# Opening of a Fourier and feed-forward kernel: R's copy on ScalarE, a weight fold moved ahead of the first product, GpSimd's sums held

## The chip, the cores and the metric

The kernel runs on 1 core of one Trainium2 chip. The metric is the device time of one execution in microseconds (us). "Span" below is the time from the first to the last instruction in the trace of one execution; the time of the same execution is some 2 us more. Every run also lists its mean granted TensorE clock, as a share of full speed.

The engines are named as in the profile: PE (TensorE), PEld (its weight loads), DVE (VectorE), ACT (ScalarE), POOL (GpSimd), SP (SyncE).

## The reference

```python
def _attn_ref(x):                      # x: 8 x 3008 x 256, float32
    X = np.fft.fft(x, axis=1)
    X = np.fft.fft(X, axis=2)
    return X.real

def _moe_ref(x, w_in, w_out):          # w_in: 256 x 2048, w_out: 2048 x 256
    h = x @ w_in
    g = h * np.cos(h)
    return g @ w_out
```

The output of the first is the input of the second, 24,064 rows.

## The kernel before

The channel transform is folded into the weights: `w_in` times a cosine matrix gives `Wc`, times a sine matrix gives `Ws` ("a fold" below, 4 passes of 128x512). The sequence transform makes, for each batch, a cosine part R and a sine part I by small DFT products; both lie in rings `Rr` and `Ir` in SBUF. A step of the feed-forward part fills a PSUM bank `H` with the contribution of one extra channel (ScalarE, `Rb` times a column of `wex`), adds `Rr` times `Wc` and `Ir` times `Ws` on TensorE, and goes on with the cosine and the second matrix. A step takes about 4.75 us on TensorE in the steady stage (from one first product to the next, as near 200 us), and some 6 to 7 us in the opening, where folds lie between. VectorE's "odd folds" are something else: sums and differences of parts of `x`, made ahead of the small DFT products.

The opening, in program order for each engine:

```python
    warm(60)                       # 60 products on ones
    ...
    fold_mm(0, 1)                  # first sine fold
    fold_mm(0, 0)                  # first cosine fold
    ...
    fold_copy(0, 1)                # ScalarE: Ws, first quarter
    take_last(0); turn_last(0)     # its last row, turned into wex[0]
    fold_copy(0, 0)
    first_x.first_part("pC")       # DFT of the extra channel
    first_R.first_part("pA")       # DFT of R, in two halves
    ...
    first_R.part(1)
    warm(6)
    fold_now("o2 O2 o1 O0 J0")     # VectorE's odd folds of x
    add_O(2, 0)
    halve_now(1, VO[3])            # the last three odd folds
    first_R.plus_copy()            # VectorE: R from PSUM into the ring
```

The rest is a list of events, each with a time, that are sorted and then issued:

```python
    for t, fn in (
        (0.5, lambda: fold_mm(1, 1)),            # second sine fold
        ...
        (0.88, lambda: first_I.early("pB", "M")),  # I's DFT
        (0.95, lambda: fold_copy(1, 1)),
        (0.955, lambda: take_last(1)),
        (0.96, lambda: turn_last(1)),            # second bias row, wex[1]
        ...
    ):
        at(t, fn)
    for k in range(4):
        at(-0.1, lambda k=k: sum_weights(0, k))  # GpSimd
    at(-1.5 * T, load_ext)                       # T is 4.8
```

Two transfers of the opening: The bias row is the last row of a folded `Ws` quarter, 512 numbers, turned on end so that each of 128 partitions gets 4 of them. It goes out from GpSimd (a software queue):

```python
    def turn_last(q):
        with nc.allow_non_contiguous_dma(reason="one row turned"):
            pin(nc.gpsimd.dma_start(out=wex[q], in_=turned[q][127:128, :]))
```

Steps 0 and 1 need `wex[0]`, steps 2 and 3 need `wex[1]`, and so on. The other transfer takes one channel of `x` for every row of every batch, element by element, from SyncE; GpSimd's memset of `x1` goes ahead of it:

```python
    def load_ext():
        x1 = spool.tile([128, HALF + 1], FP, tag="rx", bufs=1, name="x1")
        ...
        pin(nc.gpsimd.memset(x1[0 : 4 * NB, 0:768], 0.0))
        ...
        with nc.allow_non_contiguous_dma(reason="one channel"):
            copy(rows[1][:, 0:1], HALF, [[SEQ * ND, NB], [-HALF * ND, 2], [1, 1]])
            copy(rows[0][:, 0:768], 0, [[HALF * ND, 2 * NB], [ND, 768], [1, 1]])
            copy(rows[1][:, 1:768], HALF - 1, [[HALF * ND, 2 * NB], [-ND, 767], [1, 1]])
```

Later, near 115 and 134 us, that extra channel gets its own small DFT, twice ("the extra-channel part"):

```python
    def clear_ext():
        ps = state["ext"] = bank("H")
        pin(nc.vector.memset(ps[0:40, 0:NQ], 0.0))
    ...
        at(s * T + 2.905, clear_ext)
        at(s * T + 4.75, lambda: dft_ext(kodd))
        at((s + 1) * T + 1.46, lambda: ext_side(kodd))
```

## Time and profile before

| | before |
|---|---|
| time, median of 3 runs (range) | 1936.52 us (1935.99 to 1937.42) |
| span and clock of the profiled run | 1931.7 us, 0.998 |
| first product with R, with I (PE's timeline) | 33.49, 40.88 us |
| products with R of steps 1, 2, 3 | 43.56, 49.73, 57.02 us |
| granted clock | 0.5 for 3.41 us twice (from 21.1 and from 34.75 us) |

The prediction below shows the views that carry it. The first is a row of the table of stretches (stretch, length, busy time of PE, PEld, DVE, ACT, POOL, granted clock, DMA share, GB/s):

```profile
40.00:60.00 20.00, 18.43 (x62) 11.06 (x61) 13.56 (x20) 14.64 (x26) 13.61 (x19) 1.00 1.67 5
```

The DMA share is the highest of the opening while only 5 GB/s move: this is the element-by-element load. PE is idle for 1.6 us of the 20.

The second is the timeline of the kernel before (start, duration, engine, line, operation, out<-in, count; in brackets the idle time ahead of it and what ended that). SPq rows are SyncE's DMA issues:

```profile
25.61 0.63 POOL L348 DMA_DIRECT2D wex<-wl  x1 [2.43 <-ACT wl L310]
31.08 17.53 SPq L156 DMA_DIRECT2D x<-in_x_dram  x3
31.24 0.99 ACT L310 ACTIVATE H<-Rb,wex 128x256 f32<-128x256 f32 x2 [1.75 <-DMA wex<-wl]
39.73 0.58 POOL L348 DMA_DIRECT2D wex<-wl  x1 [5.58 <-ACT wl L310]
48.69 0.99 ACT L310 ACTIVATE H<-Rb,wex 128x256 f32<-128x256 f32 x2 [1.52 <-DVE G L304]
49.73 1.13 PE L298 MATMUL H<-Rr,Wc 128*128 128x256 f32 x4
```

The first bias row goes out at 25.61, and ScalarE's fill for step 0 waits for it until 31.24. The second goes out at 39.73, while SyncE is still issuing the element loads (31.08 to 48.6). The trace also keeps the moments at which the 16 parts of a transfer land; the last part of the second row lands at 48.61. ScalarE's fill for step 2 starts at 48.69, and the product with R that needs it at 49.73. The profile puts the fill's wait down to VectorE; in the program the fill waits for an earlier use of its bank by VectorE, done at 45.86, and for this row. The instruction that it names, VectorE's subtraction `G<-E,H` of step 1, ended at 48.67, but it reads the bank of step 1, which is still in use at 51.49. ScalarE's own wait instruction for the row's semaphore stands at 48.63 in the trace. So it was the row.

PE's timeline at the extra-channel part:

```profile
114.96 0.49 PE L298 MATMUL H<-MC,xe 95*40 95x95 f32 x4 [0.76 <-DVE H L722]
116.23 1.18 PE L298 MATMUL H<-MC,xe 95*40 95x95 f32 x12 [0.78 <-DVE xe L375]
133.75 2.10 PE L298 MATMUL H<-MC,xe 95*40 95x95 f32 x16 [1.09 <-DVE H L722]
```

PE stands still for 2.63 us in three waits, between very short products.

### The profile page before, as it was taken

The page shows a single profiled execution, that of the slowest core. Times are in us where ns is not written, and L with a number is a line of the kernel's source. Part 1 is how long each engine was busy: PE and PEld are TensorE (multiplying, and loading weights), DVE is VectorE, ACT ScalarE, POOL GpSimd, SP SyncE. Part 2 cuts the span into 40 slices and gives each one's busy share as a digit, 9 for nine tenths or more (in the row PEclk, how much of TensorE's full clock was granted, in tenths as well). Part 3 has the DMA queues.
Part 4 walks back from the last instruction along what each step waited for, and adds up shares of the span by engine and source line. Part 5 has one row for each costly group of instructions (what it writes and reads, how often), then busy time and mean ns, then how long its engine had stood idle before and what let it go on. Part 6 is the DMA issues. An engine that isn't in the chain of part 4 may idle for free.

```text
span 1931.7 us, 28919 instructions
## 1 busy us (share of the span) xinstructions
PE 1908.5 (99%) x9000; PEld 1652.0 (86%) x9000; DVE 1456.5 (75%) x2367; ACT 1519.5 (79%) x2993; POOL 1521.4 (79%) x2044
## 2 busy tenths in 40 slices
PE   8999999999999999999999999999999999999998
PEld 4778888888888888888888888888888888888887
DVE  6788877777777777777777777777777777777777
ACT  3767788888878887888778787788878887877886
POOL 5779888898888888888889898888878676555554
PEclk9999999999999999999999999999999999999999
DMA  9523311312123122311232113311122110100101
GB/s 200 39 65 69 59 40 28 65 28 56 24 48 57 36 40 45 56 35 37 43 68 33 40 23 61 52 40 32 29 30 36 19 20 17 18 12 12 22 9 25
DMA packets 259970, 80.59 MB, mean 42 GB/s; under 512 B 240393, under 2 KB 243256, under 8 KB 259816
## 3 DMA queue, kind: packets, MB, share of 16 engines
q1 hardware_dynamic: 248456, 48.65, 15.1%
q0 software_dynamic: 9184, 29.83, 8.3%
q8 instruction: 72, 1.18, 0.2%
q14 instruction: 82, 0.67, 0.1%
q10 hardware_dynamic: 2176, 0.26, 0.1%
HBM read 36.72 MB, written 24.69 MB: 32 GB/s over the span
## 4 chain that ended last, share of the span: by engine, by line
PE 87%; DVE 5%; ACT 5%; issue 1%; POOL 1%; DMA 0%; SPq 0%; DVEq 0%; POOLq 0%
PE H L298 34%; PE pC L298 15%; PE pD L298 15%; PE pB L298 15%; PE pA L298 7%; ACT G L310 1%; DVE G L845 1%; DVE G L304 1%; ACT E L310 1%; ACT M L310 1%; ACT z L310 1%; DVE v L304 1%; ACT H L310 0%; DVE M L304 0%; DVE o L375 0%
## 5 line engine op out<-in xcount | busy, mean ns | idle before, releaser
L307 POOL TENSOR_TENSOR G<-G 128x256 f32<-128x256 f32 x1500 | 1084.6, 734 | 357.8 <-DVE G L845 280.5
L845 DVE SCALAR_TENSOR_TENSOR G<-H,G 128x512 f32<-128x512 f32 x376 | 259.2, 689 | 222.0 <-ACT G L310 219.3
L304 DVE TENSOR_TENSOR G<-H,G 128x512 f32<-128x512 f32 x376 | 259.7, 691 | 216.9 <-ACT G L310 213.7
L298 PE MATMUL H<-Rr,Wc 128*128 128x256 f32 x1504 | 388.5, 381 | 3.1 <-DVE Rr L609 2.1
L298 PE MATMUL H<-Ir,Ws 127*128 127x256 f32 x1504 | 387.8, 379 | 3.5 <-ACT E L310 2.7
L298 PE MATMUL pC<-G,WT 128*128 128x256 f32 x1504 | 387.6, 380 | 0.8 <-DVE u L304 0.7
L310 ACT ACTIVATE H<-Rb,wex 128x256 f32<-128x256 f32 x752 | 359.9, 479 | 25.6 <-DVE G L845 9.8
L310 ACT ACTIVATE G<-H 128x512 int32<-128x512 f32 x376 | 223.8, 595 | 178.9 <-DVE G L304 178.0
L310 ACT ACTIVATE E<-H 128x512 f32<-128x512 f32 x376 | 223.8, 595 | 166.2 <-PE H L298 164.8
L298 PEld LDWEIGHTS H<-Ir,Ws 127*128 127x128 f32 x1504 | 283.4, 189 | 48.3 <-ACT E L310 7.3
L298 PEld LDWEIGHTS pC<-G,WT 128*128 128x128 f32 x1504 | 285.1, 190 | 43.1 <-PE H L298 1.5
L298 PEld LDWEIGHTS H<-Rr,Wc 128*128 128x128 f32 x1504 | 281.1, 190 | 44.2 <-issue 4.6
L310 ACT ACTIVATE G<-G,halfpi 128x512 f32<-128x512 f32 x376 | 269.3, 716 | 3.6 <-DVE G L304 3.4
L304 DVE TENSOR_TENSOR M<-G,M 128x512 f32<-128x512 f32 x376 | 257.6, 685 | 0.0
L304 DVE TENSOR_TENSOR G<-E,H 128x512 f32<-128x512 f32 x376 | 255.3, 679 | 1.6 <-PE H L298 1.5
L845 DVE SCALAR_TENSOR_TENSOR G<-G,M 128x512 f32<-128x512 f32 x376 | 254.4, 677 | 0.5 <-ACT M L310 0.5
L310 ACT ACTIVATE M<-M,halfpi 128x512 f32<-128x512 f32 x376 | 245.6, 653 | 0.0
L298 PE MATMUL pB<-G,WT 128*128 128x256 f32 x752 | 225.0, 381 | 1.4 <-POOL G L307 1.3
L310 ACT ACTIVATE M<-G 128x512 int32<-128x512 f32 x376 | 223.7, 595 | 0.0
L298 PE MATMUL pA<-G,w 128*128 128x256 f32 x752 | 223.7, 379 | 0.0
L298 PE MATMUL pD<-G,w 128*128 128x256 f32 x752 | 223.7, 379 | 0.0
L298 PE MATMUL pB<-G,w 128*128 128x256 f32 x752 | 223.7, 379 | 0.0
(164 smaller groups left out, 2070.9 us busy)
## 6 DMA issues: line engine op xcount, KB each, us to landing
out_dram<-ot SPq DMA_DIRECT2D x496, 32.0 KB
xl<-in_x_dram SPq DMA_DIRECT2D x64, 192.0 KB
e<-e POOLq DMA_DIRECT2D x22, 384.0 KB, 4.9
o<-o POOLq DMA_DIRECT2D x22, 381.0 KB, 4.9
out_dram<-ot SPq DMA_DIRECT2D x256, 2.0 KB
Rb<-r SPq DMA_DIRECT2D x10, 376.0 KB
w<-in_moe_w_in_dram SPq DMA_DIRECT2D x4, 512.0 KB
out_dram<-ot SPq DMA_DIRECT2D x64, 28.0 KB
```

Of the source, the lines that this page charges most:

```text
L298: nc.tensor.matmul(out_, lhsT=lhsT, rhs=rhs, start=start, stop=stop, skip_group_check=True)
L304: pin(nc.vector.tensor_tensor(out=o, in0=a, in1=b, op=op))
L307: pin(nc.gpsimd.tensor_tensor(out=o, in0=a, in1=b, op=op))
L310: pin(nc.scalar.activation(out=o, in_=i, func=func, **kw))
L845: nc.vector.scalar_tensor_tensor(out=o, in0=h, scalar=TWO_PI, in1=c, op0=ALU.mult, op1=ALU.mult)
```

## The change

It means to start the first product earlier and to shorten what lies between it and the first product with I: ScalarE copies R, so that VectorE's last folds are not ahead of it; the second sine fold takes the place of the six warming products; GpSimd's weight sums do not start while VectorE does its last folds (a copy of one element that depends on `O[3]` holds them); twelve more warming products keep the clock; a load changes its place; and the extra-channel DFT comes later, behind the next step's product, with its bank cleared on TensorE.

```diff
@@ loads
     load_mats(0)
+    load_w1(1)
     load_mats(1)
-    load_w1(1)
@@ clear_ext
-        pin(nc.vector.memset(ps[0:40, 0:NQ], 0.0))
+        whole_bank("ext")
@@ opening
-    warm(60)
+    warm(72)
 ...
     first_R.part(1)
-    warm(6)
+    fold_mm(1, 1)
+    first_R.plus_sum()
     fold_now("o2 O2 o1 O0 J0")
     add_O(2, 0)
     halve_now(1, VO[3])
-    first_R.plus_copy()
+    hold = spool.tile([128, 8], FP, tag="xg", bufs=1, name="hold")
+    pin(nc.gpsimd.tensor_copy(out=hold[0:1, 0:1], in_=O[3][0:1, 0:1]))
@@ events
-        (0.5, lambda: fold_mm(1, 1)),
+        (0.1, lambda: fold_copy(1, 1)),
+        (0.11, lambda: take_last(1)),
 ...
         (0.88, lambda: first_I.early("pB", "M")),
-        (0.95, lambda: fold_copy(1, 1)),
-        (0.955, lambda: take_last(1)),
-        (0.96, lambda: turn_last(1)),
+        (0.12, lambda: turn_last(1)),
 ...
-        at(-0.1, lambda k=k: sum_weights(0, k))
+        at(0.13, lambda k=k: sum_weights(0, k))
@@ plan_ext
-        at(s * T + 2.905, clear_ext)
-        at(s * T + 4.75, lambda: dft_ext(kodd))
-        at((s + 1) * T + 1.46, lambda: ext_side(kodd))
+        at(s * T + 5.6, clear_ext)
+        at(s * T + 5.65, lambda: dft_ext(kodd))
+        at((s + 1) * T + 2.3, lambda: ext_side(kodd))
```

(Also cut: the method `plus_copy`, which nothing calls any more.)

More of the change, by code (lines that the diff above doesn't have):

```diff
@@ L604, in plus_sum @@
                 act(self.ring[0:M, sl], self.uv[0:M, i:z])
-        def plus_copy(self):
-            M = self.M
-            for sl, i, z in self.at_up(0, 1, NU):
-                pin(nc.vector.tensor_copy(out=self.ring[0:M, sl], in_=self.uv[0:M, i:z]))
         def minus_sum(self):
```

## The prediction

> **What bounds the kernel now.** I first read the page's busy times, then a table of stages (busy time of each engine in chosen stretches), to see where TensorE is not the limit.
>
> ```profile
> PE 1908.5 (99%) x9000; PEld 1652.0 (86%) x9000; DVE 1456.5 (75%) x2367; ACT 1519.5 (79%) x2993; POOL 1521.4 (79%) x2044
> ```
>
> ```profile
> 10.00:15.00 5.00, 5.00 (x25) 2.25 (x23) 4.61 (x5) 0.44 (x2) 1.64 (x9) 1.00 0.97 254
> 15.00:20.00 5.00, 3.00 (x15) 1.29 (x13) 4.76 (x5) 0.64 (x2) 3.94 (x5) 1.00 0.95 243
> 20.00:25.00 5.00, 5.00 (x8) 1.82 (x7) 4.83 (x7) 2.63 (x4) 3.03 (x4) 0.66 1.04 270
> 25.00:30.00 5.00, 5.00 (x35) 4.58 (x35) 4.86 (x6) 2.38 (x5) 1.17 (x2) 1.00 1.08 316
> 30.00:40.00 10.00, 7.85 (x31) 4.84 (x28) 4.25 (x7) 3.76 (x7) 4.35 (x7) 0.83 1.34 205
> ...
> 200.00:1000.00 800.00, 798.67 (x3797) 702.54 (x3797) 602.77 (x989) 650.19 (x1297) 689.22 (x918) 1.00 0.23 44
> ```
>
> In the second view each row gives the stretch, its length, the busy time of PE, PEld, DVE, ACT and POOL, the granted clock, the DMA share and GB/s. From 200 to 1000 us PE is idle for 1.3 us of 800: the steady stage is pure TensorE, and this change removes no product from it. Only the opening (0 to about 57 us), and the idle spots between 60 and 160 us, can give time. In the opening PE "busy" is not progress: the early products are 60 warming products on ones, and the clock falls to 0.66 and 0.83.
>
> Next, the list of what PE waited for over the whole span. The columns are total, times, longest:
>
> ```profile
> PE H L298 <- DVE Rr L609: 2.1, 1, 2.1
> PE H L298 <- DMA w<-in_moe_w_in_dram: 2.0, 1, 2.0
> PE H L298 <- DVE H L722: 1.9, 2, 1.1
> PE pB L298 <- POOL G L307: 1.3, 2, 0.8
> PE H L298 <- DVE xe L375: 0.8, 1, 0.8
> ```
>
> Then PE's timeline, where R's first use, the second sine fold, I's DFT and I's first use follow each other:
>
> ```profile
> 29.89 1.46 PE L298 MATMUL M<-ones 128*128 128x512 bf16 x6
> 33.49 1.10 PE L298 MATMUL H<-Rr,Wc 128*128 128x256 f32 x4 [2.15 <-DVE Rr L609]
> 34.43 3.24 PE L298 MATMUL H<-w,CC 128*128 128x512 f32 x4
> 37.47 0.94 PE L298 MATMUL pB<-MC,o 95*128 95x95 f32 x4
> ...
> 38.92 0.58 PE L298 MATMUL M<-MC,o 94*128 94x95 f32 x4
> 39.33 0.83 PE L298 MATMUL M<-MC,z 94*128 94x188 f32 x4
> 40.88 1.13 PE L298 MATMUL H<-Ir,Ws 127*128 127x256 f32 x4 [0.71 <-DVE Ir L304]
> ```
>
> The chain that ended last agrees: VectorE's odd folds up to about 32.8, VectorE's copy of R (32.81 to 33.35), the first product and the fold behind it (33.49 to 37.5), I's DFT, I's sums (40.27), the first product with I (40.88). After that PE rarely waits, so **the start of the first product with I is the clock to watch**: what moves it moves the end.
>
> **What the Trainium skill says.**
> (1) "TensorE: Matmul & The Clock Gate", Part 1, The HAM clock gate: half rate after an idle window of about 3.4 us, full again after a busy one; the window runs freely. The trace agrees: cut at 21.1, 24.5, 31.3, 34.75 and 38.2, the clock is 0.51 in 21.1 to 24.5 and in 34.75 to 38.2, and 1.00 or 0.99 elsewhere; each slow window follows one in which PE was busy only 41% (17.7 to 21.1) or 38% (31.3 to 34.75). One with 79% was followed by no drop that I see.
> (2) "SBUF — State Buffer", Who interferes with whom: a VectorE instruction with two SBUF inputs contends with GpSimd instructions that read SBUF; the loser blocks. The trace agrees: a 96x512 fold takes 686 ns and 96x256 420 ns while GpSimd does small things, but the last odd folds, 96x508 and 96x254, take 1096 and 908 ns while GpSimd sums weights (from 30.71). Three of them take 2.98 us instead of about 1.6.
> (3) "TensorE: Matmul & The Clock Gate", What happens when you issue a matmul: products stay in program order. The trace shows it: I's DFT has its input at 32.9, yet starts at 37.47 behind the fold.
>
> **The change part by part.**
> (a) Warm-up 72 instead of 60. Warm products cost 0.216 us each, so 12 add 2.6 us: 17.83 + 2.6 = 20.4. The weights land at 19.8, so the folds start 0.6 late, but at full clock: 8 passes of 0.427 = 3.4 instead of 5.3, ending at 23.85 instead of 25.1. The first sine fold still ends near 22.2, and its copy on ScalarE (23.60, behind other copies) does not move. The DFT of R starts near 24.1, but its first copy waits for ScalarE until 25.94 (then 0.49), so its second half starts at 26.6 instead of 27.71: R is complete at about 28.9, 1.1 us early.
> (b) R copied by ScalarE: 0.49 us (its 128x377 copies), about 29.0 to 29.5 instead of 32.81 to 33.35 behind the last fold. But the first product also needs the bank that ScalarE fills from `wex`. That transfer landed at 31.24 (ScalarE idle 1.75 us for it), and none of its causes moves: ScalarE's turn ends at 25.32, GpSimd issues at 25.61, 5.6 us to landing. The two fills take 0.99, to 32.23. So the first product starts at about **32.35**, 1.15 us earlier, not 4.
> (c) The second sine fold goes ahead of it, into the place of the 6 warming products: 4 passes, 1.7 us, 28.9 to 30.6, in idle time. From first product to I's DFT took 37.47 - 33.49 = 3.98 us; it becomes one product, 0.95. Saving 3.0.
> (d) I's DFT took 2.80 us to I's first sum, its start at half clock. The same shapes at full clock: 1.08 (26.63 to 27.71) and 1.35 with the drain (38.92 to 40.27): 2.45. Saving 0.35.
> (e) GpSimd's sums held: the last folds end near 31.5 instead of 32.85. This is not on the path (the DFT starts at 33.3), but without it the margin would be 0.4 us. The price is late weight sums: after ScalarE's turn (34 us) eight of 0.73 us end at 40.5, before their first use (52.4 - 4.5 = 48).
> (f) Weights ahead of the second matrix: both should land near 24 to 27 (estimate from the cumulated GB/s), before use at 28.9 and 33.3. Nothing.
> (g) The extra-channel DFT later, its bank cleared on PE. Before, PE waited 0.76 + 0.78 (at 115 and 116) and 1.09 (at 133.75): 2.63 us. After, the next product goes first, once ScalarE has filled its bank (114.5 and 132.9), then a zero product (0.2). From the timelines, product plus DFT end at 117.2 instead of 118.3 and at 136.2 instead of 136.75. Saving 1.1 + 0.55, less some DVE lag: about 1.2.
> Sum: 1.15 + 3.0 + 0.35 = 4.5 in the opening (first product with I at 36.4), 1.2 later, 5.7 in all. I take off 0.4 for waits that do not shift stiffly (GpSimd is 94 to 97% busy from 146 to 176 us): 1936.5 - 5.3 = **1931.2 us**.
>
> **Rivals.**
> (R1) `wex` becomes the wait. I already count it at 31.2. If it lands 1.5 us later, the gain drops by 1.5. If its landing is tied to the load, it might come earlier: R is ready at 29.5, fold done at 30.6, so up to 1.5 us more gain, then limited by the last fold (31.5).
> (R2) The clock drops again. PE idles from 30.6 to 32.35, 1.75 us, at most 51% of a 3.4 us window; 58 to 62% idle triggered it. If it does, some 3.4 us run at half speed: 1.5 us lost. The windows run freely, so this may differ between runs. I give it one in four.
> (R3) The gain is given back: GpSimd's later sums, or the second batch's loads, which queue behind the slow one-channel loads (31.1 to 48.7 at issue; 1.5 us later now while the steps are 4.5 earlier). No wait for `xl` shows up after 60 us, and the first fold of it is at 112; GpSimd idled 5.6 us at 39.7 and 2.8 at 46.0. Little lost; at worst the total gain is 3.
> (R4) Everything was hidden and the time stays. Against it: the chain runs straight through the removed pieces, and PE never waits long afterwards.
>
> **Range and chances.** Between 1928.8 (`wex` early, the extra-channel waits all gone) and 1934.2 (clock drop plus late `wex`). 2% is 38.7 us, beyond anything the opening holds; a loss of that size would need a broken steady stage, and its program is the same. Faster 0.01, same 0.98, slower 0.01.
>
> **What would show it.** Right: the first product with Rr near 32.3 and its wait named `wex` or ScalarE; 6 warming products gone and the second sine fold near 29; the granted clock 1.00 from 20 to 30 us; the three last odd folds at about 1.6 us; the first product with Ir near 36.4; no PE wait on VectorE's memset at 115 and 134; PE idle between 200 and 1000 us unchanged. Wrong: a clock below 0.9 between 30 and 40; `wex` landing far from 31.2; new PE waits on GpSimd's sums between 45 and 160 us; or the shift at 36 us not found again at 200 us.

## The result, and the profile after

| | before | after |
|---|---|---|
| time, median (range), 4 runs each | 1936.26 us (1933.62 to 1937.42) | 1925.95 us (1923.26 to 1928.85) |
| ratio | | 0.9949 (0.9928 to 0.9970) |
| spans of the single runs | | 1921.4, 1921.8, 1926.1, 1926.8 us |
| their clocks | | 0.999, 0.999, 0.997, 0.997 |

A ratio here and below comes from the runs of both kernels in the same rounds, and is not quite the ratio of the medians quoted. The gain is 10.3 us by the medians, where 5.3 were predicted: under 2%, as expected, but outside the range of 1928.8 to 1934.2. The changed kernel has two levels, 4.9 us apart by their means, and its profiled run is one of the slower level.

From the list of what PE waited for in the first 200 us, after the change (waited for, us in total, times, longest):

```profile
PE H L298 <- ACT H L310: 2.5, 3, 1.9
PE H L298 <- DMA w<-in_moe_w_in_dram: 0.6, 1, 0.6
PE pB L298 <- POOL G L307: 0.2, 1, 0.2
```

The waits on VectorE's copy of R, on its memset and on `xe` are gone. A wait for ScalarE's fill of `H` stands in their place. The timeline after:

```profile
28.56 1.88 PE L298 MATMUL H<-w,CC 128*128 128x512 f32 x4
30.56 1.59 DVE L375 TENSOR_TENSOR o<-o 96x508 f32<-96x508 f32 x3
31.27 0.99 ACT L310 ACTIVATE H<-Rb,wex 128x256 f32<-128x256 f32 x2 [2.02 <-DMA wex<-wl]
32.31 1.52 PE L298 MATMUL H<-Rr,Wc 128*128 128x256 f32 x4 [1.86 <-ACT H L310]
33.62 1.01 PE L298 MATMUL pB<-MC,o 95*128 95x95 f32 x4
34.20 0.56 POOL L348 DMA_DIRECT2D wex<-wl  x1 [1.13 <-ACT wl L310]
38.76 2.08 PE L298 MATMUL H<-Ir,Ws 127*128 127x256 f32 x4 [0.71 <-DVE Ir L304]
46.88 0.98 ACT L310 ACTIVATE H<-Rb,wex 128x256 f32<-128x256 f32 x2
48.77 1.03 PE L298 MATMUL H<-Rr,Wc 128*128 128x256 f32 x4
```

The second sine fold runs at 28.56; the last odd folds take 1.59 us instead of 2.98; the fill waits for the first bias row until 31.27; the first product with R starts at 32.31 (predicted 32.35). Then each product takes twice its time (2.08 us for the four with I instead of 1.13), and the first one with I starts at 38.76, not at 36.4. The second bias row goes out at 34.20 instead of 39.73, and the fill for step 2 (46.88) waits for nothing. The table of stretches, after:

```profile
20.00:25.00 5.00, 4.93 (x16) 2.54 (x17) 4.72 (x8) 2.70 (x4) 2.96 (x4) 1.00 1.05 239
30.00:40.00 10.00, 7.42 (x25) 6.08 (x24) 4.02 (x9) 4.61 (x8) 7.32 (x12) 0.65 1.27 220
40.00:60.00 20.00, 20.00 (x66) 12.95 (x66) 13.21 (x20) 15.58 (x27) 10.97 (x15) 0.92 1.62 4
200.00:1000.00 800.00, 798.67 (x3798) 702.67 (x3797) 600.16 (x986) 650.51 (x1297) 689.15 (x918) 1.00 0.24 44
```

The clock is kept from 20 to 25 us (0.66 before), but from 30 to 40 it is 0.65. The steady stage is the same to the hundredth: 798.67 us of 800. Cut at the clock's own windows of 3.41 us, the slow part reads:

```profile
29.46:32.87 3.41, 1.54 (x6) 0.66 (x5) 3.27 (x8) 1.53 (x4) 1.49 (x3) 1.00 1.07 393
32.87:36.28 3.41, 3.41 (x14) 3.23 (x13) 0.25 (x1) 1.94 (x3) 2.19 (x5) 0.51 1.11 239
36.28:39.70 3.42, 2.71 (x9) 2.11 (x9) 1.01 (x2) 1.14 (x3) 3.34 (x6) 0.50 1.59 70
39.70:43.11 3.41, 3.41 (x6) 1.69 (x5) 2.18 (x4) 1.25 (x3) 0.84 (x2) 0.50 1.79 4
```

PE was busy for 1.54 us of the window that ends at 32.87, which is 45%, and the next three windows ran at half clock, 10.24 us. The window from 32.87 counts as 100% busy and still did not end it; its products are mostly the short ones of I's DFT (95 and 188 columns). The window of long products (39.70 to 43.11) did. That the short products are the reason is not shown.

So two questions are open. Even with 10.24 us at half clock, the kernel gained more than predicted: from what? And what is the gain where the clock is kept?

### The profile page after: what moved, and what is told of

The parts are those of the page before. It is cut to its first block, busy times and chain, and to the rows that moved or that the text cites. A ratio compares the mean times of both kernels' runs of the same rounds, so it can differ in the third digit from the quotient of the medians.

```text
span 1926.1 us, 28934 instructions
## 1 busy us (share of the span) xinstructions
PE 1908.7 (99%) x9007; PEld 1655.0 (86%) x9008; DVE 1451.3 (75%) x2364; ACT 1519.5 (79%) x2994; POOL 1521.6 (79%) x2045
## 4 chain that ended last, share of the span: by engine, by line
PE 89%; ACT 4%; DVE 3%; issue 1%; POOL 1%; DMA 0%; POOLq 0%; DVEq 0%; ACTq 0%
PE H L298 35%; PE pC L298 16%; PE pD L298 16%; PE pB L298 15%; PE pA L298 8%; ACT G L310 1%; DVE G L840 1%; DVE G L304 1%; ACT E L310 1%; ACT z L310 1%; ACT M L310 1%; DVE v L304 1%; ACT H L310 0%; DVE M L304 0%; POOL xl L182 0%
## 5 line engine op out<-in xcount | busy, mean ns | idle before, releaser
L298 PE MATMUL pD<-G,WT 128*128 128x256 f32 x752 | 223.7, 379 | 0.0
```

Of the source, the lines that this page charges most:

```text
L298: nc.tensor.matmul(out_, lhsT=lhsT, rhs=rhs, start=start, stop=stop, skip_group_check=True)
```

## The experiments

All kernels gave correct results. "Before" is the run of the kernel before on the same chip in the same rounds. Spans matter more than times where clocks differ, so both are given.

| run | time (median), its spans | before | ratio (95%) |
|---|---|---|---|
| e1_after | 1924.81; 1921.2 to 1923.5 | 1937.26 | 0.9933 (0.9920 to 0.9947) |
| e2_fill | 1923.92; 1921.6 to 1924.2 | 1937.26 | 0.9935 (0.9921 to 0.9948) |
| e3_ext_only | 1931.64; 1928.1 to 1932.1 | 1937.26 | 0.9973 (0.9959 to 0.9987) |
| e4_no_ext | 1932.84; 1926.3 to 1932.1 | 1937.26 | 0.9968 (0.9955 to 0.9982) |
| e5_i_first | 1923.81; 1921.2 to 1922.1 | 1936.48 | 0.9936 (0.9920 to 0.9953) |
| e6_late_row | 1931.53; 1926.3 to 1930.4 | 1936.48 | 0.9974 (0.9957 to 0.9990) |
| e10_dve_clear | 1923.45; 1921.4 to 1921.8 | 1936.48 | 0.9936 (0.9919 to 0.9952) |
| e11_before_fill | 1935.72; 1931.4 to 1934.2 | 1936.48 | 0.9996 (0.9979 to 1.0012) |
| e8_no_hold | 1924.07; 1922.0 to 1922.4 | 1937.69 | 0.9933 (0.9917 to 0.9950) |
| e9_r_dve | 1923.70; 1921.2 to 1922.2 | 1937.69 | 0.9931 (0.9914 to 0.9947) |
| e12_fold_only | 1934.98; 1928.4 to 1934.3 | 1937.69 | 0.9983 (0.9964 to 1.0002) |
| e13_flood_later | 1931.42; 1928.8 to 1930.2 | 1937.69 | 0.9972 (0.9955 to 0.9989) |
| e14_fold_fill | 1929.56; 1927.3 to 1927.8 | 1935.80 | 0.9968 (0.9952 to 0.9985) |

The runs that share a value of "before" ran on one chip, e14_fold_fill on another. Each kernel has four or five executions, the kernel before seven or nine in each group.

### The clock: the change again, and with fillers

`e1_after` is the changed kernel once more, in later rounds.

> The changed kernel itself, again. Four runs so far lie at two levels: spans 1926.1 and 1926.8 us with a mean clock of 0.997, and 1921.4 and 1921.8 us with 0.999. Theory C (clock): TensorE idles about 2 us before the first product with R; where a window of the clock gate falls badly on it, some 10 us run at half rate and the run is 5 us longer. Expected: two levels again, some 5 us apart, each run's level told by its mean clock (0.997 against 0.999), and a profile with a clock of 0.5 for about 10 us only in a run of the longer level. Rival D (the small transfer for the bias row lands late in some runs): the level would not follow the clock, and the first product with R would start at 32.3 us in one level and near 37 in the other.

The two levels that were expected did not come again. The five spans lie between 1921.2 and 1923.5 at clocks of 0.998 and 0.999: none shows the slower level, and the profiled one keeps the clock at 1.00 through the opening, with the first product with I at 36.95. Together with the first four, 2 of 9 executions dropped. `e4_no_ext` below has the same opening and belongs here too: its profile shows the same 10.24 us at half clock, from 33.21, and 3 of its 5 executions list clocks of 0.995 to 0.997. So 3 to 5 of 14 dropped; in which stage the two unprofiled ones of e4 lost their clock is not known.

`e2_fill` puts nine warming products into PE's idle time ahead of the first product:

```diff
     fold_mm(1, 1)
+    warm(9)
     first_R.plus_sum()
```

> The changed kernel with 9 warming products (9 x 0.216 = 1.9 us) between the second sine fold and the first product with R, where TensorE idled 1.9 us. They add work to TensorE and nothing else. Theory C expects: clock 1.00 throughout the opening, one level only, span 1921 to 1922 us (time about 1923.5), all runs within 1.5 us. The first product with R still starts near 32.3 us, the first product with I near 36.4 us instead of 38.8. Rival D expects the two levels to stay. If the fillers only delay the first product, the time is 0 to 1 us longer than the short level.

```profile
32.46 1.03 PE L298 MATMUL H<-Rr,Wc 128*128 128x256 f32 x4
36.38 1.13 PE L298 MATMUL H<-Ir,Ws 127*128 127x256 f32 x4 [0.71 <-DVE Ir L304]
44.63 1.03 PE L298 MATMUL H<-Rr,Wc 128*128 128x256 f32 x4
```

With the clock kept, the first product with I starts at 36.38; the prediction said 36.4. That it fits to the tenth is partly luck: in this profile the first bias row landed early, at 30.43, ScalarE's fill was done at 31.50, and it was the nine fillers that held the first product until 32.46. In e1, without fillers, the row landed at 31.81 and the two products start at 32.93 and 36.95. What is confirmed is the distance between them, 3.9 to 4.0 us (4.05 predicted), and that a far slower start (38.76) is the clock. But look at the last line of the view: the product with R of step 2 starts at 44.63, 5.1 us earlier than before (49.73), and that of step 3 is 5.9 earlier (51.10 against 57.02). A stiff shift of 4.5 doesn't give that. In the five kernels with fillers at this place (e2, e8, e9, e10, and e5 with four), 21 executions were timed, and all list a clock of 0.999 or 1.000, where 3 to 5 of 14 without fillers dropped. The theory of the clock stands. The spread expected for e2 (1.5 us) was missed: its times lie within 2.6 us, and one span, 1924.2 at a clock of 0.999, has no explanation. Nor are the fillers a gain over e1's executions, none of which dropped: on the same chip the means are 1924.4 us for both.

### The extra-channel part: alone, and left out

`e3_ext_only` is the kernel before with the extra-channel part of the diff alone (the bank cleared on TensorE, the three event times); `e4_no_ext` is the changed kernel without them (the same diff, backwards).

```diff
-        pin(nc.vector.memset(ps[0:40, 0:NQ], 0.0))
+        whole_bank("ext")
...
-        at(s * T + 2.905, clear_ext)
-        at(s * T + 4.75, lambda: dft_ext(kodd))
-        at((s + 1) * T + 1.46, lambda: ext_side(kodd))
+        at(s * T + 5.6, clear_ext)
+        at(s * T + 5.65, lambda: dft_ext(kodd))
+        at((s + 1) * T + 2.3, lambda: ext_side(kodd))
```

> The kernel before with only the later part of the change: the extra channel's bank cleared on TensorE, its DFT one step position later. The prediction sized this at 1.2 us. In the two profiles the waits for VectorE's memset and folds (2.7 us) and for GpSimd's sums (1.3 to 0.2 us) fall by 3.8 us, less two zero products of about 0.2 us: theory E expects 3.3 us less than before, with the waits at 115, 116 and 134 us gone. The prediction's own working expects 1.2 us.

> The changed kernel with the extra channel's part undone (memset on VectorE, DFT at the old position): the opening's part alone. Theory E expects 3.3 us more than the changed kernel at the same clock level (spans near 1924.8 and 1929.6 us); the prediction's working expects 1.2 us more.

In the changed kernel the two DFTs run behind the next step's product, without the waits for `xe` and the memset (PE's timeline of after):

```profile
112.75 1.13 PE L298 MATMUL H<-Rr,Wc 128*128 128x256 f32 x4 [0.37 <-ACT H L310]
114.13 1.51 PE L298 MATMUL H<-MC,xe 95*40 95x95 f32 x16
130.40 2.13 PE L298 MATMUL H<-MC,xe 95*40 95x95 f32 x16
```

Alone, the part takes 0.27% of 1937 off, about 5.2 us (0.13 to 0.41%, so 2.5 to 7.9), where 3.3 were expected and 1.2 predicted; the clocks of both kernels vary in these runs. Left out, the profiled run has the waits again (1.9 us on VectorE's memset in two, 0.8 on `xe`, 1.3 on GpSimd in two), and the two best spans, at a kept clock of 0.999, are 1926.3 and 1927.4: 4.3 to 5.4 above the profiled run of e2. The trace of the changed kernel tells where the gain comes in. Taking the start of the first output product of every step, before minus after, the lead is constant at 1.83 us up to 110 us (this run had the slow windows), jumps by 0.9 at the first extra-channel DFT, by 1.65 at the second, and grows in the steps behind them to 5.76: 3.9 in all. The same reckoning between other profiles gives the same: 3.97 from before to e3, 3.91 from before to e2, 3.9 from e4 to e2. So 3.9 us is what the part is worth at the same clock. The growth behind the DFTs goes with a lag of VectorE and GpSimd: in the kernel before, VectorE waited 2.12 us for ScalarE up to 120.1 us, and PE then waited twice for GpSimd (0.49 and 0.81); of these two PE waits 0.2 us are left after the change.

`e10_dve_clear` takes e2_fill and gives the clearing back to VectorE at its old time, while the DFT stays at its new place:

```diff
-        whole_bank("ext")
+        pin(nc.vector.memset(ps[0:40, 0:NQ], 0.0))
...
-        at(s * T + 5.6, clear_ext)
+        at(s * T + 2.905, clear_ext)
         at(s * T + 5.65, lambda: dft_ext(kodd))
```

> The filled kernel with the extra channel's bank cleared by VectorE's memset at the old place in its order, but the DFT at the new place. Tells the two halves of that part apart. If the place of the DFT (behind the next product with R instead of ahead of it) is what gains, the time is within 0.5 us of e2_fill (span 1922.0), as the memset at 114.4 us is done before the DFT. If the memset is what costs, the span is 2 us or more longer, with TensorE waiting for the memset at about 111 and 128 us.

1923.45 us, the ratio of e2_fill: with the DFT at its new place, which engine clears the bank, and when, is worth nothing. The new times of the DFT and of `ext_side` behind it carry the gain; these two were not taken apart.

### The second bias row

Where does the rest of the lead at step 2 and 3 come from? By now two theories stood against each other. Theory W: the second bias row, turned behind the second sine fold, lands earlier, and step 2 waited for it. Theory C: the kernel before lost it to the clock. `e6_late_row` takes e2_fill and sends the row at its old place in GpSimd's order, behind the weight sums:

```diff
-        (0.12, lambda: turn_last(1)),
+        (0.99, lambda: turn_last(1)),
```

> The filled kernel (e2_fill) with one transfer moved: GpSimd issues the second bias row (the second wex transfer, 2 KB) behind its eight weight sums, near 40.3 us, instead of ahead of them at 33.5. In the kernel before it was issued at 39.7 us, in the middle of the flood of one-channel loads, and landed at 48.6; ScalarE's fill for step 2 then started at 48.7, though the profile names VectorE. Theory W (that landing cost the kernel before 1.5 us in the opening, which the prediction took as a stiff shift): the row lands near 49 us, 8 to 9 us after issue, the step-2 product with R starts near 49.6 instead of 44.6 us, and the time is 3 to 5 us longer than e2_fill's. The prediction's stiff shift expects no change (below 0.5 us).

```profile
49.24 0.99 ACT L310 ACTIVATE H<-Rb,wex 128x256 f32<-128x256 f32 x2 [7.18 <-DMA wex<-wl]
50.28 2.08 PE L298 MATMUL H<-Rr,Wc 128*128 128x256 f32 x4 [5.87 <-ACT H L310]
```

The first product with I stays at 36.00, yet step 2's product with R waits 5.87 us and starts at 50.28, later than in the kernel before. The profile now names the row. The kernel loses 8.1 us by the medians, where 3 to 5 were expected, to e10_dve_clear (which ran on the same chip and is as fast as e2_fill), some of it to the slow clock behind this wait (6.83 us at half clock in the profiled run). Everything that was gained in the opening is lost again by one transfer of 2 KB.

`e11_before_fill` tries theory C: the kernel before with 72 and 16 warming products.

```diff
-    warm(60)
+    warm(72)
...
-    warm(6)
+    warm(16)
```

> The kernel before with its clock kept up: 72 warming products instead of 60, and 16 instead of 6 ahead of the first product with R; no other change. Theory C (clock): the runs of the kernel before lie between spans of 1931.2 and 1937.5 us with mean clocks of 0.998 to 0.995, because of two to four slow windows of 3.41 us. Filled, all runs should have 0.999, span near 1929.5 (two slow windows cost some 1.7 us each in its profile of 1931.7, the second gap of 2.1 us being filled), spread below 2 us. Then the rest of the change, at a kept clock, is worth 1929.5 - 1922 = 7.5 us or a little more. Rival: the fillers make no difference, and the spread of the kernel before has another cause.

This expectation failed. The opening's clock was kept and the first product with I moved from 40.88 to 39.33, but the time is that of the kernel before:

```profile
38.48 0.58 POOL L348 DMA_DIRECT2D wex<-wl  x1 [4.22 <-ACT wl L310]
49.73 0.99 ACT L310 ACTIVATE H<-Rb,wex 128x256 f32<-128x256 f32 x2 [4.33 <-DMA wex<-wl]
50.77 1.13 PE L298 MATMUL H<-Rr,Wc 128*128 128x256 f32 x4 [3.02 <-ACT H L310]
```

The row went out 1.25 us earlier than before and landed 1 us later, at 49.65: the opening's gain ran into a floor. So the row gates the kernel before at step 2, whatever is gained ahead of it.

Why does 2 KB take 11 us? `e13_flood_later` takes e11 and moves the element-by-element loads behind the issue of the row, by the memset that precedes them:

```diff
-    at(-1.5 * T, load_ext)
+    at(0.97, load_ext)
```

> The kernel before with more fillers (72 and 16 warming products, as in the run that kept the opening clock and gained nothing), and the three element-wise loads of the one channel moved behind the issue of the second bias row, by GpSimd's memset ahead of them, some 10 us later. Theory that the flood of these loads is what delays the row: it lands 4 to 6 us after its issue at 38.5 instead of 11.2, near 43.5; ScalarE's 3 us wait at step 2 and PE's slow window behind it are gone, step 2's product with R near 47 instead of 50.8, and the time is 3 to 4 us under the kernel before, near 1932.5, unless the third and fourth rows, which now lie in the flood, are late for steps 4 and 6. Rival (the row's landing is slow by itself, or because of its 128 little pieces): landing still 9 to 11 us after issue, and the time of the run without the move, 1935.7.

```profile
38.79 0.58 POOL L348 DMA_DIRECT2D wex<-wl  x1 [4.90 <-ACT wl L310]
40.15 12.30 SPq L156 DMA_DIRECT2D x<-in_x_dram  x3
45.60 0.98 ACT L310 ACTIVATE H<-Rb,wex 128x256 f32<-128x256 f32 x2
47.90 1.03 PE L298 MATMUL H<-Rr,Wc 128*128 128x256 f32 x4
```

The row lands at 40.77, 1.98 us after its issue, less than I had expected. ScalarE's wait and the slow window behind it are gone. One line moved took the ratio from 0.9996 (e11) to 0.9972, which is some 4.6 us; between the two profiles the lead at step 3 is 4.67. The flood of element-by-element loads is the cause of the late landing, and this is shown by the run; how it holds the row up is not. All profiles side by side, with the landing of the last of 16 parts:

| profile | row issued | landed | took | step 2's product with R |
|---|---|---|---|---|
| before | 39.73 | 48.61 | 8.9 | 49.73 |
| e3_ext_only | 40.26 | 50.76 | 10.5 | 51.89 |
| e11_before_fill | 38.48 | 49.65 | 11.2 | 50.77 |
| e6_late_row | 38.99 | 49.16 | 10.2 | 50.28 |
| after | 34.20 | 41.63 | 7.4 | 48.77 (slow clock) |
| e1_after | 34.82 | 41.93 | 7.1 | 45.21 |
| e2_fill | 33.46 | 40.94 | 7.5 | 44.63 |
| e14_fold_fill | 34.07 | 42.54 | 8.5 | 45.70 |
| e13_flood_later | 38.79 | 40.77 | 2.0 | 47.90 |

In five more profiles of kernels with the row's early place (e4, e5, e8 to e10) the transfer took 5.8 to 7.0 us. In the upper four rows of the table, the product follows the landing by 1.1 us each time; in the lower five it does not depend on it.

### The opening taken apart

`e12_fold_only` is the kernel before with the second sine fold moved, alone:

```diff
-    warm(6)
+    fold_mm(1, 1)
...
-        (0.5, lambda: fold_mm(1, 1)),
-        (0.95, lambda: fold_copy(1, 1)),
-        (0.955, lambda: take_last(1)),
-        (0.96, lambda: turn_last(1)),
+        (0.1, lambda: fold_copy(1, 1)),
+        (0.11, lambda: take_last(1)),
+        (0.12, lambda: turn_last(1)),
```

> The kernel before with one part of the change alone: the second sine fold goes ahead of the first product, in the place of the six warming products, and with it the copy of the fold and the turning of the second bias row come some 3 to 5 us earlier. R is still copied by VectorE behind its last odd fold, GpSimd's sums are not held, the warm-up is 60, the extra-channel DFT is at its old place. My theory (the fold's place carries the opening, by two effects: 3.0 us less on TensorE between the first product and I's DFT, and the second bias row issued near 34 instead of 39.7, so that it lands near 41 to 42 instead of 48.6): first product with R still near 33.5, first product with I near 37.5 (40.9 before), step 2's product with R near 46 (49.7 before), time 4 to 5 us less than the kernel before, near 1931.5, the whole opening but 1.5 us. Rival (the copy of R on ScalarE and the longer warm-up carry a third of it or more): 2 us less or fewer.

The expectation was missed, 1934.98 instead of 1931.5 (one execution of four, at a clock of 0.998, took 1930.39). The timeline of PE, and two of the clock's windows:

```profile
33.63 2.05 PE L298 MATMUL H<-Rr,Wc 128*128 128x256 f32 x4 [3.70 <-DVE Rr L609]
```

```profile
29.48:32.89 3.41, 0.45 (x2) 0.00 (x0) 3.31 (x4) 1.11 (x3) 3.21 (x5) 1.00 1.08 353
32.89:36.30 3.41, 2.67 (x9) 2.34 (x9) 1.56 (x5) 2.07 (x3) 2.92 (x5) 0.50 1.28 141
```

Without R's copy on ScalarE, and without the fillers, PE waits 3.70 us for R. The clock's window from 29.48 has PE busy for 0.45 us of 3.41, and 13.65 us at half clock follow, until 46.5. The first product with I starts at 40.60, as before the change. The row landed at 43.33, and was not waited for. So the run says nothing of the fold's worth, and I repeated it with the clock kept: `e14_fold_fill` is e12 with a warm-up of 72 and twelve warming products behind the fold.

```diff
-    warm(60)
+    warm(72)
...
     fold_mm(1, 1)
+    warm(12)
```

> The run with the second sine fold's place alone changed was ruined by a clock drop of 13.65 us behind PE's wait of 3.70 us for R. Here the same kernel, with fillers: a warm-up of 72, and twelve warming products behind the fold, so that PE's wait shrinks to about 1 us and the granted clock stays at 1.00 in the opening. My theory (the fold's place carries the opening once the clock is kept; the copy of R and the held sums only keep PE's idle gap short): first product with R near 33.5, first product with I near 37.5, second bias row landed near 41 to 43, step 2's product with R at 45.7 to 46.5, span 1926 to 1928.5, time 1928 to 1930.5, so 5 to 6 us less than the same kernel with the fold at its old place and fillers (1935.7), and what is left to the full change with fillers (1923.9) is the 3.9 us of the extra-channel part and 1 us of the opening. Rival (the copy on ScalarE and the held sums are worth more than 1 us by themselves): 1931.5 or more at a kept clock.

```profile
33.46 1.10 PE L298 MATMUL H<-Rr,Wc 128*128 128x256 f32 x4 [0.66 <-DVE Rr L609]
37.44 1.13 PE L298 MATMUL H<-Ir,Ws 127*128 127x256 f32 x4 [0.71 <-DVE Ir L304]
45.70 1.03 PE L298 MATMUL H<-Rr,Wc 128*128 128x256 f32 x4
```

This met the expectation at every point: I at 37.44, step 2 at 45.70, spans of 1927.3 to 1927.8. Against the same fillers with the fold at its old place (e11), the first product with I is 1.9 us earlier and step 2 is 5.1. The fold's place, with the earlier row that comes with it, carries most of the opening; the rest of the change brings step 2 1.07 us further forward (44.63 in e2). The profile has one slow window left, and it lies behind the extra-channel waits, which this kernel still has:

```profile
108.89:112.31 3.42, 1.88 (x18) 1.29 (x16) 3.32 (x7) 1.75 (x4) 3.01 (x5) 1.00 0.25 37
112.31:115.72 3.41, 3.41 (x11) 2.63 (x9) 0.76 (x2) 1.14 (x3) 1.33 (x2) 0.50 0.58 107
```

A window with PE 55% busy (1.88 of 3.42 us, and with short products) was enough here. The profile of e12 has a slow window of this kind too, from 118.2 us. No profile of a kernel with the extra-channel part at its new place (after, e1, e2, e3, e5, e6, e8, e9, e10) shows one after 60 us. Of six profiles with the part at its old place (before, e4, e11, e12, e13, e14) two show it. So the part at its new place seems also to take away a chance of losing some 1.7 us (half of 3.41).

`e8_no_hold` and `e9_r_dve` undo one part each of e2_fill: the sums not held, and R copied by VectorE.

```diff
-    hold = spool.tile([128, 8], FP, tag="xg", bufs=1, name="hold")
-    pin(nc.gpsimd.tensor_copy(out=hold[0:1, 0:1], in_=O[3][0:1, 0:1]))
...
-        at(0.13, lambda k=k: sum_weights(0, k))
+        at(-0.1, lambda k=k: sum_weights(0, k))
```

> The changed kernel with nine fillers ahead of the first product (the version that kept the clock, 1923.9 us), and GpSimd's weight sums not held: the four sums are back at their old place, beside VectorE's last odd folds. As predicted (the hold is not on the path): the last three odd folds take 2.9 to 3.0 us in sum again instead of 1.6 to 2.0, end near 32.9 instead of 31.5 to 32, I's DFT waits 0 to 0.4 us for them, first product with I at 36.4 to 36.8, and the time is 0 to 0.5 us more: 1923.9 to 1924.4. Rival (the hold is worth its name): 1.2 us or more lost. A third way: without the hold the sums are done earlier and GpSimd has room, so the time is a little less, and the row turned behind them goes out at the same time.

```diff
-    first_R.plus_sum()
...
     halve_now(1, VO[3])
+    for sl, i, z in first_R.at_up(0, 1, NU):
+        pin(nc.vector.tensor_copy(out=first_R.ring[0:128, sl], in_=first_R.uv[0:128, i:z]))
```

> The changed kernel with nine fillers ahead of the first product, and R copied by VectorE behind its last odd fold again, as before the change, the sums still held. As predicted (the first product waits for the first bias row anyway, so R's copy on ScalarE gains only what lies between the last fold and the fills): R ready near 32.3 to 32.8 instead of 30, first product with R near 32.8 to 33.0 instead of 32.5, first product with I near 36.4 to 36.9, time 0 to 0.5 us more, 1923.9 to 1924.4. Rival (the copy on ScalarE is what gains): 1 us or more lost.

Both are nothing: 1924.07 and 1923.70 us. Without the hold the last three odd folds take 2.98 us again and end at 33.22, and I's DFT still starts on time at 33.28. With R on VectorE the copy ends at 32.30, and the first product starts at 32.45, held by ScalarE's fill (0.23 us) and so by the first bias row. So each of the two is worth nothing alone once fillers keep the clock. But they stand in for each other: e14, which has neither, copies R behind folds that take 2.99 us, and starts the first product at 33.46, held by that copy, 1.0 us after e2. Without fillers, e12, which also lacks the longer warm-up, has PE idle for 3.70 us where the changed kernel has 1.86.

### A candidate

`e5_i_first` goes further than the change: I's DFT ahead of the first product, into the wait for the first bias row, with the copies of the fold earlier on ScalarE and four warming products.

```diff
-        (0.1, lambda: fold_copy(1, 1)),
-        (0.11, lambda: take_last(1)),
-        (0.88, lambda: first_I.early("pB", "M")),
-        (0.97, first_I.copy_e),
+        (-1.95, lambda: fold_copy(1, 1)),
+        (-1.94, lambda: take_last(1)),
+        (-0.05, lambda: first_I.early("pB", "M")),
+        (0.05, first_I.copy_e),
```

> A candidate for a better version: the changed kernel, 4 fillers, and I's DFT ahead of the first product with R (which waits for the first bias row until 31.2 us and ScalarE's fill until 32.2, while I's folds are ready at 31.5); the second sine fold's copy and row ahead of the fill on ScalarE. DFT from 31.6 to 34.0, first product with R at 34.0, I's sums at 34.3, first product with I at 35.8 (held by ScalarE's doubled copy of the bank) instead of 36.4. Expected: 0.6 us less than e2_fill, span 1921.4; if the product with R at 34.0 delays more than it gains, the same or 0.5 us more.

No gain: 1923.81 us. The first product with I starts 0.4 us earlier (35.95), but PE now waits for ScalarE's copy `E` twice (0.69 and 0.56 us), and step 2's product with R is at 44.62, where e2_fill has 44.63. The best versions are e2_fill and e10_dve_clear; they show no slower level in the runs taken. Against e1, whose runs show none either, the mean of e2 on the same chip is the same (1924.4 us).

## Why the prediction was wrong, point by point

**Right.** Step (a) and (b): the first product with R waits for the first bias row through ScalarE's fill and starts at 32.35 by the prediction, at 32.31 to 32.93 in three profiles (in e2 held by the fillers, so there the fit is luck). Step (c) and (d): the first product with I at 36.4, and at 36.38 and 36.95 where the clock is kept. Step (e): the hold shortens the folds to 1.59 us (they start 0.65 us later than before, and end at 32.15, not 31.5) and gains nothing by itself (e8). Step (f), the load's new place, shows nothing in the profiles; it was not run alone. The steady stage did not change. The rival R1 was counted rightly. The whole gain lies where the prediction looked, and stays below 2%.

**The step that failed in the opening** is "the start of the first product with I is the clock to watch: what moves it moves the end". The prediction priced the first bias row carefully and never asked for the second. In the kernel before, step 2 stood at 49.7 because that row landed at 48.61, so the end did not hang on the first product with I alone. e11 shows it: 1.5 us won there were worth nothing. The change moves the row's issue by 5.5 us as a side effect, out of step 2's way, and the lead at step 3 is 5.9 us instead of 4.5. The prediction had both rows of the profile within reach, the fill at 48.69 after a wait of 1.52 us and the row's issue at 39.73; it priced the first row at its measured 5.6 us and did not look for the second. Its own last sign of being wrong came true: the lead at I is not the lead at 200 us (4.5 and 9.9 us from before to e2, 2.1 and 5.75 from before to the profiled run of after).

**The term that was mis-sized** is (g), the extra-channel DFT, with 1.2 us: it measured 3.9 us at the same clock in the traces (5.2 us in e3 by the ratio, with its wide interval). The prediction counted TensorE's own gain at the two places as 1.1 + 0.55 and took something off for VectorE's lag. The two places gave 0.8 + 1.65, and the lag went the other way: the other 1.5 us came in the steps behind, where VectorE and GpSimd were no longer late.

**The sum.** Between two profiled runs, before and e2, the span went from 1931.7 to 1922.0, which is 9.7. The terms are 4.5 for the opening as predicted, 1.4 for the second row (5.9 less 4.5) and 3.9 for the extra channel: 9.8. Against the predicted 5.3 the difference is 4.4: 1.4 that no step of the prediction had, 2.7 that (g) was too small, and the 0.4 that it took off.

**The base.** The prediction subtracted a gain read from one profile from the median of all runs. But the profiled run of before (1933.6 us) was among its fastest: clock 0.998, where most executions of the kernel list 0.995 to 0.997 and some 1935 us of span. By estimate, a slow window of 3.41 us lowers the mean clock by 0.5 x 3.41 / 1931 = 0.0009 and costs about 1.7 us, so these runs had up to three windows more than the profiled one. The changed kernel on a good run has none in the opening. That difference, 2.6 us from the median of before to its profiled run, was in the gain and in no step. The two slow executions of after took about as much away again: its median lies 2.4 us above its two good ones. So the 10.3 us of the medians is close to the 9.7 of the good profiles by chance. Where before's extra windows lie was not profiled; e11, e12 and e14 show two places that have them, behind the wait for the second row and behind the extra-channel waits.

**The rival R2** was named, with the right cause and nearly the right chance (one in four; 2 of 9, with e4 3 to 5 of 14). The sign that it set, a clock below 0.9 between 30 and 40 us, came (0.65). Its size was wrong: not 3.4 us at half clock and 1.5 us lost, but 10.24 us and 4.9 us; the first slow window did not bring the clock back. It worked against the gain: the medians differ by 10.3 us with two such runs of four, and by 12.5 us in e1, where no run dropped.

**Open:** which of the windows with a PE share near 50% drop the clock. Cutting the 15 kept profiles at their own windows of 3.41 us (without the kernel's end) narrows it: all 8 full-clock windows in which PE was busy 42% or less were followed by half clock, and none with 60% or more was. Between 45 and 55% three were (after 45%, e12 and e14 55%) and four were not (e13 45%, e1 54%, before and e4 55%). So the busy share alone does not decide there. In e1, PE idled for 2.12 us in one piece with no drop, in the profiled run of after for 1.86 with one.

## What to carry to other kernels

Before a shift is carried to the end of the span, follow each later consumer in the opening back to its own transfer: a 2 KB row can be the floor, and then what is won ahead of it is lost at it. Send small urgent transfers ahead of element-by-element loads; in e13, the order alone took the landing from 11.2 to 2.0 us and the kernel 4.6 us down. Before you subtract a gain from a median, check that the profiled run has the median's clock, and put fillers where PE idles for half a clock window or more; here none of 21 executions with fillers showed the level 4.9 us slower, and the fillers cost nothing that the means show.

## What the Trainium skill lacked or had wrong

- "TensorE: Matmul & The Clock Gate", Part 1, The HAM clock gate, gives half rate after an idle window and full rate after a busy one. The traces show the clock dropping after windows with PE up to 55% busy (1.54 of 3.41 us in after, 1.88 of 3.42 in e14), and staying at half through a window that counts 100% busy with products of 95 and 188 columns: 10.24 us in after and e4, 13.65 us in e12. The page has no threshold of PE's share for either way: here 42% or less always dropped the clock, 60% or more never, and 45 to 55% did both.
- "DMA: Bandwidth & Descriptors", section "SWDGE vs HWDGE vs iDMA", says that the two kinds of queue feed different queues inside each DMA engine, and that the engine takes turns between them. A reader may then expect a small software-queue transfer to pass beside a busy hardware queue. Here the second row, 2 KB, took 5.8 to 11.2 us within the element-by-element loads, and 1.98 us ahead of them (the first row of before took 5.5 us beside large loads at 316 GB/s); the page has no figure for a small transfer beside such loads.
- The same page, "Rules for kernel authors", says that a non-contiguous last dimension lowers to one descriptor per element. The trace agrees: from 30 to 70 us the kernel before has 24,837 packets of 4 bytes on SyncE's queue, and the DMA share is 1.67 at 5 GB/s from 40 to 60 us. The page doesn't say that this also delays other small transfers, which was the costlier part here.
- No page that I found warns that the releaser of a wait can be misnamed when a DMA's landing ends it: in the profile of before the fill's wait of 1.52 us is put down to VectorE, whose instruction ended at 48.67, 0.06 us after the row landed, but on another bank; the same wait in e11 (4.33 us) is put down to the row.
